# Weight preparations in units 2 to 108 of an attention and MLP kernel, each placed by an offset of its own

## The chip, the cores and the metric

The kernel runs on one core of one Trainium2 chip. The metric is the device time of one execution in microseconds (us). Five engines work side by side, each through its own instructions in order: TensorE (PE in the profile, its weight loads PEld), VectorE (DVE), ScalarE (ACT), GpSimd (POOL) and SyncE (SP), which here only issues DMAs. ACT issues some DMAs too.

## What is computed

An adaLN-conditioned block: attention over the last 512 keys of a cache (32 query heads, 16 key/value heads, head size 128), then a gated MLP. S = 2048 rows, D = 576, F = 4608, all in float32.

```python
x = A_x
mod = (_silu(c) @ w_mod).reshape(c.shape[0], 6, 1, -1)
sa, ca, ga, sb, cb, gb = (mod[:, 0], mod[:, 1], mod[:, 2], mod[:, 3], mod[:, 4], mod[:, 5])
h = _layernorm(x, axis=-1) * (1 + ca) + sa
x = x + ga * _A_ref(h, A_k_cache, A_v_cache, A_wq, A_wo)
h = _layernorm(x, axis=-1) * (1 + cb) + sb
x = x + gb * _B_ref(h, B_W_gate, B_W_up, B_W_down)
...
q = (lambda x, *d: x.transpose(*d))((x @ wq).reshape(B, Sq, Hq, Dh), 0, 2, 1, 3)
scores = jnp.einsum("bhqd,bhkd->bhqk", q, k) * (Dh ** -0.5)
p = _softmax(scores, axis=-1)
o = jnp.einsum("bhqk,bhkd->bhqd", p, v)
...
gate = gate * (lambda x, dt: x.astype(dt))(gate > 0, gate.dtype)
h = gate * up
```

## The kernel before

**Numbers.** Every product is made with operands split in two: a high part (a cast to fp32r, on ACT) and a low part (the difference, on POOL). A product is then three matmuls: high by high, low by high, high by low. So each weight matrix must be *prepared* before it is used.

**Units.** Attention runs as 128 units (UNITS), one for each head and block of 512 query rows; the eight units of a group g share keys and values g and use heads 2g and 2g + 1. In the last five groups each group comes twice, with two blocks each time (VIS). In unit u TensorE does, in this order: 12 score matmuls (s, L496 to L498), 14 matmuls for the query projection of unit u + 1 (qps, L424), a piece of the output projection (wo, L660, 12 matmuls of 288 columns), 12 matmuls of probabilities by values for unit u - 1 (pv, L633 to L635), another piece. The MLP follows.

**The other engines in a unit.** DVE takes maxima of the scores (L501), spreads them (L571), subtracts (L591), makes the low part of the next query (qlo, L480), a partial row sum (ks, L606) and the head's output (L641). ACT makes the next query's high part (qhi, L476), copies a finished piece out of PSUM (acc, L669) and seeds the next one (L693; there is one such PSUM buffer), takes the exponential (L593) and makes the high part of p (hi, L577). POOL finishes the row sum (ks, L609) and makes the low part of p (lo, L600). The output of unit u - 2 is split in high (ohi, ACT L645) and low (olo, POOL L649): at place 0 of an even unit, after place 3 of an odd one. A piece that needs a pair of heads starts at place 6 of the odd unit, behind olo.

**Places.** Everything that isn't part of a unit's fixed order is a step with a time t = 10 u + k: unit u, place k (0 to 9). `run(u, k)` emits all steps up to that time. The program order of each engine's instructions follows from it. Places 0 to 4 come before the first half of the exponential, 5 between the halves, then come ks on DVE and POOL, then 6 and 7, the head's output on DVE, 8, lo on POOL, and 9. A step's time is where it stands in the order, not a clock: an engine reaches it when it is through with what is ahead.

**Preparations.** `prep` makes two or three steps of one: `.l` issues the load on SP into one of two raw buffers, `.g` (output weights only) multiplies by the gate row on DVE (L223), `.c` cuts (ACT L182, POOL L183) into one of three buffers of its kind: wA for q, wB for k and v, wC for o. HOOK allows places 0, 4, 6 and 9, and the load stands a fixed number of hooks ahead of the cut. Group g has q(2g), k(g), q(2g+1), v(g), o(2g), o(2g+1). `park...` are those of the late groups, prepared early and stored to DRAM by `keep` (a DMA from ACT); `again` loads a stored one back on SP. Steps m3 to m5 load and add rows of the modulation (DVE L130), with their own buffers (xm). `w_later` builds sums of the MLP's weights from a layout in DRAM: a load of two tiles, one or more combinations on POOL (L943), between them a reload of the second tile on SP (L933), then a cut (ACT L950, POOL L951 and L953), then a store from ACT (L752). The names are wP60 for P6, first half, and so on; P6 has two combinations. SP also issues many copies that make that layout (wlay, L1459).

Of the kernel before, what the change touches and what calls it, by code (L numbers as in the profile page):

```python
# [23 lines left out]
EPS = 1e-5  # L24
SCALE = float(P) ** -0.5
H2 = D // 2
PLAN = {'a1.st0': -14, 'a1.nm0': -15, 'a1.st1': -14, 'a1.nm1': -15, 'a1.st2': -14, 'a1.nm2': -15, 'a1.st3': -14, 'a1.nm3': -15, 'a1.rs': -15, 'a1.tr0': -15, 'a1.af0': -11, 'a1.tr1': -15, 'a1.af1': -15, 'a1.tr2': -15, 'a1.af2': -15, 'mods': -3}
CFG = {'a0': (('s', 'vvp', 'vvv'), ('m', 'aap', 'avp'), ('w', 'aav')), 'a1': (('w', 'aap', 'vap'), ('m', 'vvp', 'vvv'), ('s', 'avp'))}
PE0, PE1, MLP0 = 4, 1, 8
# [5 lines left out]
def kernel(  # L35
# [106 lines left out]
    def mod_row(j, r, plus):  # L142
# [70 lines left out]
    def prep_out(d, k, src, key, slot=None, at=(None, "wC")):  # L213
# [11 lines left out]
        def cut():  # L225
# [12 lines left out]
    hb = {(qb, d): dr.tile([2, 4, 32, 512] if d == 4 else [P, 512], F32, name=f"hb{qb}_{d}")  # L238
          for qb in range(NQB) for d in range(5)}
# [32 lines left out]
    class LayerNorm:  # L272
# [4 lines left out]
        def stats(self, i):  # L277
# [205 lines left out]
    st_, t5, pt, hi_, lo_, bc, rb, ks_, pvps, done, o, bps = ({} for _ in range(12))  # L483
# [167 lines left out]
    def down_piece(his, los, ws, i, qt, nm, pool=None, seed=None):  # L651
# [3 lines left out]
        for half in range(2):  # L655
            cs = slice(half * H2, (half + 1) * H2)
            n = 0
            for hi, lo, w in zip(his, los, ws):
                for a, b in ((hi, 0), (hi, 1), (lo, 0)):
                    nc.tensor.matmul(ps[:, half, :H2], a[:, sl], w[b][:, cs],  # L660
                                     start=(n == 0 and seed is None), stop=(n == 5),
# [746 lines left out]
    live = {"q": wqs, "k": ks, "v": vs, "o": wos}  # L1408
# [365 lines left out]
```

## Time and profile before

| what | value |
|---|---|
| median of 3 runs | 2860.26 us (2857.57 to 2861.42) |
| the profiled execution | 2857.6 us, span 2855.8 us |
| mean granted TensorE clock | 0.998 |
| instructions | 41174 |
| DMA | 399.57 MB, 140 GB/s on average |

A row of the timeline reads: start in us from the span's start, duration in us, engine, line of the kernel, operation, tile written <- tiles read, shapes, count; in brackets the idle time before it and what ended that. A row of the waits reads: who waited <- for whom, us in total, times, longest. Busy time of TensorE is modelled and matmuls overlap, so rows of 0.39 us start 0.23 us apart.

### The profile page before, as it was taken

Reading aid. Unit: us, or ns where it says so; the run is one execution under the profiler, and the core shown is the slowest. Engines: PE = TensorE matmul, PEld = TensorE weight load, DVE = VectorE, ACT = ScalarE, POOL = GpSimd, SP = SyncE. Lnnn points to the kernel's source line nnn. Section 1 sums busy time; section 2 is a strip of 40 time slices with the busy share of each in tenths; the row PEclk is TensorE's granted clock in tenths of the full one; section 3 lists DMA queues with packets and bytes.
Section 4 is the critical chain, followed back from the end, with each engine's and each line's share of the span. In section 5 each row is a group of like instructions: output and inputs, shape, how many; then the busy total and the mean of one; then the engine's idle time right before and its main releaser. Section 6 shows DMA issues by size and latency. Waiting matters only on the chain.

```text
span 2855.8 us, 41174 instructions
## 1 busy us (share of the span) xinstructions
PE 2815.0 (99%) x15006; PEld 2449.5 (86%) x15006; DVE 2246.8 (79%) x3384; ACT 1476.7 (52%) x2105; POOL 2123.8 (74%) x1564
## 2 busy tenths in 40 slices
PE   6999999999999999999999999999999999999999
PEld 5788888888888888888888888888888888888888
DVE  7899999999889998888889756676677466666666
ACT  5766666666766666666656444444444122222221
POOL 5688888888899989877778766788777356656653
PEclk9999999999999999999999999999999999999999
DMA  4012132222232213312243456666667844444442
GB/s 163 24 45 79 65 106 85 83 82 100 95 104 94 92 62 131 105 70 80 68 155 139 150 213 229 231 240 231 234 234 261 338 165 154 155 155 159 159 154 106
DMA packets 164506, 399.57 MB, mean 140 GB/s; under 512 B 15056, under 2 KB 62160, under 8 KB 164304
## 3 DMA queue, kind: packets, MB, share of 16 engines
q1 hardware_dynamic: 132912, 284.69, 29.9%
q10 hardware_dynamic: 31392, 112.26, 10.0%
q8 instruction: 118, 1.93, 0.3%
q14 instruction: 84, 0.69, 0.1%
HBM read 271.16 MB, written 154.57 MB: 149 GB/s over the span
## 4 chain that ended last, share of the span: by engine, by line
PE 83%; DVE 6%; POOL 5%; issue 2%; ACT 2%; DMA 2%; SPq 0%; ACTq 0%; DVEq 0%; POOLq 0%
PE gu L1016 26%; PE wo L660 12%; PE qps L424 11%; PE md L660 8%; PE st_P L1118 6%; PE s L498 3%; PE s L497 3%; PE s L496 3%; PE pv L635 3%; PE pv L634 3%; PE pv L633 3%; POOL lo L600 2%; DVE t L501 1%; DVE p L591 1%; POOL wop L795 1%
## 5 line engine op out<-in xcount | busy, mean ns | idle before, releaser
L600 POOL TENSOR_TENSOR lo<-p,hi 128x1024 fp32r<-128x1024 f32 x256 | 610.6, 2406 | 1.1 <-ACT hi L577 1.1
L609 POOL TENSOR_TENSOR ks<-ks,p 128x512 f32<-128x512 f32 x256 | 351.7, 1374 | 238.7 <-DVE ks L606 135.5
L501 DVE TRANSPOSE_TENSOR_REDUCE t<-s 128x32 f32<-128x1024 f32 x256 | 313.8, 1239 | 85.9 <-PE s L498 76.6
L1016 PE MATMUL gu<-hop_B,wop 128*128 128x512 f32 x1512 | 375.0, 391 | 0.2 <-POOL wop L795 0.2
L1016 PEld LDWEIGHTS gu<-hop_B,wop 128*128 128x128 f32 x1512 | 274.9, 188 | 51.1 <-POOL wop L795 0.9
L1016 PE MATMUL gu<-hop_T,wop 128*128 128x512 f32 x1260 | 316.1, 391 | 0.0
L424 PE MATMUL qps<-hTa,wA 128*128 128x512 f32 x1288 | 312.9, 394 | 3.1 <-DVE hTa L372 1.6
L660 PE MATMUL wo<-woga,ohi 128*128 128x288 f32 x1472 | 298.8, 295 | 2.0 <-POOL woga L183 1.4
L591 DVE TENSOR_TENSOR p<-s,mb 128x1024 f32<-128x1024 f32 x246 | 290.3, 1219 | 4.2
L424 PEld LDWEIGHTS qps<-hTa,wA 128*128 128x128 f32 x1288 | 244.5, 190 | 56.6 <-DVE hTa L372 3.2
L476 ACT ACTIVATE qhi<-qps 128x512 fp32r<-128x512 f32 x128 | 76.4, 597 | 366.9 <-PE qps L424 358.4
L660 PEld LDWEIGHTS wo<-woga,ohi 128*128 128x128 f32 x1472 | 245.9, 188 | 18.8 <-POOL woga L183 3.4
L1016 PEld LDWEIGHTS gu<-hop_T,wop 128*128 128x128 f32 x1260 | 227.8, 188 | 39.0
L577 ACT CAST hi<-p 128x1024 fp32r<-128x1024 f32 x256 | 259.5, 1042 | 1.5
L660 PE MATMUL md<-wogb,hhi 128*128 128x288 f32 x1272 | 256.9, 295 | 0.4 <-DVE acc L671 0.4
L593 ACT ACTIVATE p<-p 128x1024 f32<-128x1024 f32 x246 | 249.5, 1051 | 13.7 <-DVE p L591 13.4
L671 DVE TENSOR_TENSOR acc<-md,acc 128x576 f32<-128x576 f32 x159 | 119.9, 755 | 160.4 <-PE md L660 159.8
L660 PEld LDWEIGHTS md<-wogb,hhi 128*128 128x128 f32 x1272 | 210.9, 188 | 12.6 <-DVE acc L671 1.4
L1127 DVE TENSOR_TENSOR acc<-st_P,acc 128x576 f32<-128x576 f32 x160 | 121.1, 757 | 127.9 <-PE st_P L1118 127.9
L660 PE MATMUL wo<-woga,olo 128*128 128x288 f32 x736 | 217.8, 296 | 1.3 <-POOL olo L649 1.2
L660 PE MATMUL md<-wogb,hlo 128*128 128x288 f32 x636 | 187.5, 295 | 0.0
L649 POOL TENSOR_TENSOR olo<-rb,ohi 128x512 fp32r<-128x512 f32 x128 | 167.4, 1308 | 15.2 <-ACT ohi L645 15.0
(283 smaller groups left out, 7095.3 us busy)
## 6 DMA issues: line engine op xcount, KB each, us to landing
wop<-wk_P SPq DMA_DIRECT2D x133, 640.0 KB
wk_P<-wop ACTq DMA_DIRECT2D x119, 640.0 KB
wr<-wlay SPq DMA_DIRECT2D x68, 384.0 KB
rogb<-wd SPq DMA_DIRECT2D x68, 288.0 KB
againq<-akq SPq DMA_DIRECT2D x18, 640.0 KB
rwA<-wq SPq DMA_DIRECT2D x32, 320.0 KB
wlay<-wg SPq DMA_DIRECT2D x36, 256.0 KB
roga<-wo SPq DMA_DIRECT2D x32, 288.0 KB
```

What stands on the lines that cost most here:

```text
L424: return [lambda i=i, a=a, b=b: nc.tensor.matmul(ps, a, b, start=(i == 0), stop=(i == n - 1)) for i, (a, b) in enumerate(ops)]
L501: nc.vector.tensor_reduce(t5[u][:, 2 * h:2 * h + 2, :].rearrange("p k b -> p (k b)"), t.rearrange("p k (b j) -> p (k b) j", j=32), axis=AX ...
L577: nc.scalar.copy(hi_[u, h], pt[u, h])
L591: nc.vector.tensor_tensor(p, t, bc[u][:, None, :].to_broadcast([P, 2, 512]), op=ALU.subtract)
L593: nc.scalar.activation(p, p, AF.Exp, bias=0.0, scale=1.0)
L600: nc.gpsimd.tensor_sub(lo_[u, h], pt[u, h], hi_[u, h].bitcast(F32))
L609: nc.gpsimd.tensor_tensor(ks_[u], ks_[u], p[:, j, :], op=ALU.add)
L649: nc.gpsimd.tensor_sub(olo[u], o.pop(u), ohi[u].bitcast(F32))
L660: nc.tensor.matmul(ps[:, half, :H2], a[:, sl], w[b][:, cs], start=(n == 0 and seed is None), stop=(n == 5), skip_group_check=seed is not None)
L1016: nc.tensor.matmul(ps, a, c, start=s not in heir(m) and i == 0 and s not in seeds_of(m), stop=i == len(ops) - 1, skip_group_check=True)
L1118: nc.tensor.matmul(ps[:, j, :H2], x[:, sl], w[:, y, :], start=n == 0 and not second, stop=n == 2, skip_group_check=True)
L1127: nc.vector.tensor_tensor(t, ps[:, :, :H2], t, op=ALU.add)
```

## The change

Each step's time gets an offset of its own from a table OFF of 280 entries, by name; names that aren't in it get 0. So that every step has a name, keep, again, park and the steps of `w_later` are given ones with their weight (and for `w_later` their time). Nothing else changes: the same instructions, buffers and loops. Offsets lie between -24 and +20, that is up to two units and a half; most are between -6 and +6. The last steps moved are at 1060 to 1070.

```diff
+OFF = {'keepo24_0': 10, 'q5.l': 5, 'q5.c': -3, 'parkq25.l': 1, 'q8.c': -9, 'parko25.l': 3, 'parko25.g': -4, 'parko25.c': -3,
...
+ 'o5.g': 2, 'o9.g': -3, 'q11.l': 7, 'q11.c': 12, 'q10.c': 11, 'q12.c': 5, 'o14.l': 7, 'q18.c': -8, 'o17.l': -10, 'o17.g': -10,
...
+ 'wP11.576': -2, 'parkq30.c': -1, 'wP41.656': -1, 'k7.c': -5, 'keepk14_0': 20, 'o16.l': 1, 'o16.g': -6, 'parko28.l': 10,
+ 'parko29.l': 7, 'parko29.c': -4, 'o19.g': -3, 'o20.g': -6, 'o20.c': -9, 'o22.c': 5,
...
+ 'wP60.796': 17, 'wP60.804': 9, 'wP61.824': 14, 'wP61.836': 12, 'wP61.844': 15, 'wP61.856': 3, 'k11.c': -1,
...
+ 'm5.l': -1, 'gb': 1}
...
     def step(name, t, fn, *args):
-        sched.append((t + PLAN.get(name, 0), len(sched), fn, args))
+        sched.append((t + PLAN.get(name, 0) + OFF.get(name, 0), len(sched), fn, args))
...
-        step("keep", t, lambda: keep(key, d[k][2] if key[0] == "o" else
+        step(f"keep{key[0]}{key[1]}_{int(t >= 1000)}", t, lambda: keep(key, d[k][2] if key[0] == "o" else
...
-                step("again", B + t, again, key, live[key[0]], key[1],
+                step(f"again{i}{key[0]}{key[1]}", B + t, again, key, live[key[0]], key[1],
...
-                prep("park", B + t, pr, gap)
+                prep(f"park{key[0]}{key[1]}", B + t, pr, gap)
...
-                step("w.l", t, fn)
+                step(f"w{s}{xx}.{t}", t, fn)
```

The steps that the prediction names, with their times before and after (worked out from the code and the table):

| step | before | after |
|---|---|---|
| parkq30.c, cut of wP11 (name wP11.576) | 576, 576 | 575, 574 |
| parkq31.c, cut of wP41 (wP41.656) | 656, 656 | 656, 655 |
| q10.c, q12.c, q18.c, o22.c | 369, 449, 689, 889 | 380, 454, 681, 894 |
| o9.g, parko25.g, o19.g | 350, 360, 750 | 347, 356, 747 |
| o5.g, o16.g, o20.g | 190, 646, 806 | 192, 640, 800 |
| o20.c | 809 | 800 |
| wP60: two combinations, cut | 796, 804, 816 | 813, 813, 816 |
| wP61: load, two combinations, cut | 824, 836, 844, 856 | 838, 848, 859, 859 |
| k11.c | 860 | 859 |
| q11.c | 386 | 398 |
| keep of k14, k7.c | 513, 540 | 533, 535 |
| o14: load, gate | 559, 566 | 566, 566 |
| o16: load, gate | 639, 646 | 640, 640 |
| parko28: load, gate | 589, 600 | 599, 600 |
| parko29: load, gate | 669, 680 | 676, 680 |

More of the change, by code (lines that the diff above doesn't have):

```diff
@@ L26 @@
 H2 = D // 2
+OFF = {'keepo24_0': 10, 'q5.l': 5, 'q5.c': -3, 'parkq25.l': 1, 'q8.c': -9, 'parko25.l': 3, 'parko25.g': -4, 'parko25.c': -3, 'm4.0.l': -16, 'm4.0.c': -1, 'k3.l': -4, 'parkq26.l': -6, 'o7.l': -1, 'parkq27.l': 12, 'hb.r': -15, 'o5.g': 2, 'keepq27_0': 3, 'v4.c': 2, 'keepk12_0': -6, 'q9.l': -13, 'm4.1.l': -18, 'q10.l': -6, 'parkq26.c': -2, 'q8.l': -14, 'parkv12.l': -3, 'm3.4.l': 1, 'o9.g': -3, 'k3.c': -11, 'm3.3.c': -2, 'o7.g': -3, 'm4.2.l': -5, 'parkk12.l': -18, 'parkk13.l': -6, 'parkk13.c': -10, 'o6.l': 2, 'm3.2.l': 4, 'q6.c': 10, 'm3.1.l': 9, 'o4.c': 4, 'q6.l': 17, 'm3.1.c': -2, 'parko24.g': -1, 'keepk13_0': -12, 'k2.l': 4, 'q11.l': 7, 'k5.c': 12, 'q7.l': 12, 'k4.l': -18, 'v3.l': 5, 'v2.c': -4, 'm4.2.c': -3, 'k4.c': -1, 'keepq25_0': 18, 'keepo25_0': 3, 'm4.4.l': 7, 'keepv12_0': -2, 'v2.l': -4, 'q10.c': 11, 'm3.3.l': 2, 'v4.l': -21, 'keepq26_0': -1, 'o8.l': -1, 'o8.g': 1, 'q9.c': 3, 'o9.l': 3, 'o5.l': -12, 'v5.l': -1, 'o6.c': 14, 'k2.c': 3, 'parkv12.c': -6, 'q4.c': 2, 'm3.2.c': 19, 'q7.c': 8, 'm4.1.c': -2, 'q11.c': 12, 'parkq27.c': 3, 'o7.c': -1, 'parko24.l': -9, 'm4.3.c': 1, 'o6.g': 2, 'm3.pad': 2, 'm4.3.l': -18, 'parko24.c': 13, 'm3.4.c': -1, 'o9.c': -1, 'k6.l': 2, 'k6.c': -3, 'parko28.l': 10, 'parko28.c': -1, 'v7.l': 6, 'wP20.596': -1, 'o13.g': -4, 'wP11.564': 5, 'keepv14_0': 3, 'wP11.576': -2, 'm5.1.l': -13, 'm5.4.c': -2, 'q15.l': -13, 'wP21.604': 10, 'keepk14_0': 20, 'parko26.l': 3, 'parko26.g': -2, 'parko26.c': -5, 'v6.l': -4, 'q14.c': -5, 'parkq29.l': 3, 'o13.l': -18, 'm5.st': -9, 'q16.l': -24, 'm5.4.l': -18, 'keepq29_0': 14, 'o15.l': -12, 'keepo27_0': 11, 'm4.col': -3, 'keepo26_0': 14, 'parkq28.l': -4, 'parkq28.c': 2, 'k7.c': -5, 'parkq29.c': 1, 'q13.l': -6, 'q13.c': -2, 'q16.c': 12, 'm5.2.l': 4, 'v5.c': 1, 'm5.3.l': -7, 'm5.1.c': -3, 'q12.c': 5, 'keepo28_0': 6, 'parkv13.l': -3, 'parkq30.l': -6, 'keepq30_0': -2, 'keepq28_0': 16, 'q12.l': -7, 'm5.0.l': -8, 'q15.c': -4, 'k8.l': -1, 'o12.l': -2, 'o15.g': -4, 'o15.c': -5, 'm5.0.c': -10, 'wP10.546': -19, 'wP10.556': -10, 'o10.c': 4, 'keepv13_0': 8, 'o14.l': 7, 'k7.l': 4, 'parko27.l': 6, 'parkk14.l': -3, 'parkq30.c': -1, 'parkk14.c': -2, 'q14.l': -1, 'parkv13.c': -1, 'o10.l': -9, 'o14.c': -2, 'parkv14.l': 2, 'o11.g': -1, 'o12.c': -2, 'm5.3.c': -1, 'o12.g': 1, 'o11.l': 1, 'parko27.c': -2, 'wP50.744': -7, 'wP60.796': 17, 'wP70.684': 1, 'keepv15_0': 7, 'parkk15.l': 3, 'parkk15.c': -3, 'q17.c': 5, 'wP61.844': 15, 'wP61.824': 14, 'wP61.836': 12, 'o20.l': -14, 'o20.g': -6, 'o20.c': -9, 'parko31.l': -4, 'parko31.g': -3, 'parko31.c': -2, 'parkv15.l': -9, 'wP51.776': -2, 'o21.l': -9, 'o21.g': -1, 'o21.c': -1, 'o19.c': -1, 'parko29.l': 7, 'v10.c': 4, 'wP50.736': -2, 'q22.l': 1, 'q19.l': -12, 'o17.g': -10, 'wP41.644': 2, 'k10.l': -4, 'k10.c': 3, 'wP41.656': -1, 'q19.c': -11, 'q20.c': 6, 'o17.l': -10, 'wP71.704': -3, 'k9.c': -1, 'v9.l': 8, 'v9.c': -1, 'wP71.716': 2, 'k9.l': -8, 'q18.c': -8, 'v10.l': -5, 'wP40.624': 2, 'wP51.756': 2, 'q21.l': 4, 'o19.l': 2, 'v8.l': -5, 'keepk15_0': 5, 'keepo30_0': 7, 'parko30.c': 6, 'o16.c': 1, 'q20.l': -5, 'keepo29_0': 5, 'wP70.676': -2, 'o18.g': 1, 'o16.g': -6, 'parko29.c': -4, 'q18.l': -6, 'wP51.764': 1, 'o19.g': -3, 'keepq31_0': -4, 'q21.c': 6, 'parko30.l': 1, 'parkq31.l': 5, 'o16.l': 1, 'wP21.616': 2, 'o18.c': 2, 'q17.l': 8, 'again15k15': 7, 'v11.l': -6, 'v11.c': -1, 'again13v13': -10, 'again14v14': -3, 'wP31.924': 7, 'again15q31': 5, 'again14o29': 3, 'q23.l': 10, 'q23.c': 4, 'again14o28': 6, 'again13q26': 1, 'again13o26': 1, 'again13o27': 3, 'again15o30': -13, 'again15q30': 12, 'keepo31_0': -5, 'o23.l': -3, 'again13q27': -10, 'again14q28': 12, 'keepo23_0': 1, 'again12q25': -4, 'keepq23_0': 7, 'again14k14': 6, 'again15o31': 1, 'keepo22_0': 16, 'wP31.944': 3, 'q22.c': 3, 'wP31.916': 3, 'wP30.896': -1, 'keepq22_0': 4, 'again16k11': -5, 'o22.l': 7, 'again14q29': -6, 'again12k12': -3, 'keepv11_0': -3, 'again12q24': -11, 'k11.l': -7, 'again16q22': -8, 'o22.c': 5, 'm5.l': -1, 'again13k13': -1, 'again12o25': -11, 'again16q23': 4, 'wP61.856': 3, 'wP31.956': -6, 'k11.c': -1, 'gb': 1, 'wP30.884': 6, 'wP60.804': 9}
```

## The prediction

> **What bounds the kernel now.** I read the page first, for which engine is full, then the waits of TensorE, for what still interrupts it.
>
> ```profile
> PE 2815.0 (99%) x15006; PEld 2449.5 (86%) x15006; DVE 2246.8 (79%) x3384; ACT 1476.7 (52%) x2105; POOL 2123.8 (74%) x1564
> ```
>
> ```profile
> PE wo L660 <- POOL woga L183: 1.4, 3, 0.7
> PE wo L660 <- POOL olo L649: 1.2, 5, 0.5
> PE pv L635 <- POOL lo L600: 1.1, 2, 0.6
> PE s L498 <- DVE qlo L480: 0.9, 2, 0.7
> ```
>
> TensorE is busy 99% of the span, so the change cannot shorten its work; it can only remove interruptions or add some. The few there are come late from POOL or DVE: low parts of weights (L183), of heads' outputs (L649), of probabilities (L600) and of queries (L480). To see how much there is to win, I take from the timeline of TensorE the first score matmul of a unit.
>
> ```profile
> 134.73 0.39 PE L496 MATMUL s<-qhi,kv 128*128 128x512 f32 x1
> 146.56 0.39 PE L496 MATMUL s<-qhi,kv 128*128 128x512 f32 x1
> ```
>
> ```profile
> 745.38 0.39 PE L496 MATMUL s<-qhi,kv 128*128 128x512 f32 x1
> ```
>
> ```profile
> 770.81 0.39 PE L496 MATMUL s<-qhi,kv 128*128 128x512 f32 x1
> ```
>
> ```profile
> 841.87 0.39 PE L496 MATMUL s<-qhi,kv 128*128 128x512 f32 x1
> ```
>
> ```profile
> 866.73 0.39 PE L496 MATMUL s<-qhi,kv 128*128 128x512 f32 x1
> ```
>
> ```profile
> 1307.56 0.39 PE L496 MATMUL s<-qhi,againk 128*128 128x512 f32 x1
> ```
>
> These are the starts of units 7, 8, 58, 60, 66, 68 and 105. Unit 7 is undisturbed: 146.56 - 134.73 = 11.83 us. Units 7 to 104 take 1172.83 us, 98 times 11.83 is 1159.3, so **13.5 us (0.5%) is all that can be won here**. Units 58 and 59 take 25.43, 1.77 too long; 66 and 67 take 24.86, 1.20 too long; the other 10.5 us lie scattered, part of them in a few added matmuls.
>
> **What the change takes away.** No instruction is added or removed; each engine gets the same ones in another order. The cause of the longest pair stands in POOL's timeline.
>
> ```profile
> 745.37 2.67 POOL L609 TENSOR_TENSOR ks<-ks,p 128x512 f32<-128x512 f32 x2 [1.39 <-ACT p L593]
> 748.00 1.57 POOL L183 TENSOR_TENSOR wA<-rwA,wA 128x640 fp32r<-128x640 f32 x1
> 749.53 0.45 POOL L951 TENSOR_TENSOR wb_P<-wa_P,wb_P 32x128 fp32r<-32x128 f32 x1
> 749.95 0.73 POOL L953 TENSOR_TENSOR wa_P<-wa_P,wb_P 128x256 fp32r<-128x256 f32 x1
> 750.64 4.74 POOL L600 TENSOR_TENSOR lo<-p,hi 128x1024 fp32r<-128x1024 f32 x2
> ```
>
> Work at place 6 of a unit (parkq30.c and a cut of w_later, both at 576) comes after ks, which waited 1.39, and ahead of lo: 1.57 + 0.45 + 0.73 = 2.7 us that delay lo. At 575 and 574 it stands ahead of ks and uses that idle time. So units 58 and 59 lose their 1.77. In 66 and 67 only the cut moves ahead (656 to 655), the other stays: I count 1.0. In units 37, 45, 69 and 89 a cut (1.57 for a query's) stands just ahead of olo of an odd unit, which a piece needs at once; 369 goes to 380, 449 to 454, 689 to 681, 889 to 894, all clear of that spot. Gates move from place 0 to 6 or 7 (350 to 347, 360 to 356, 750 to 747), where this trace shows them cheaper:
>
> ```profile
> 638.17 0.75 DVE L223 TENSOR_TENSOR roga<-roga,mrow 128x576 f32<-128x576 f32 x1
> ```
>
> ```profile
> 663.12 1.52 DVE L223 TENSOR_TENSOR roga<-roga,mrow 128x576 f32<-128x576 f32 x1
> ```
>
> The first ran at place 6, the second at place 0 beside POOL's ks. The waits for olo and qlo (0.5 and 0.7 the longest) are what these moves address: I count 0.6 for each of the four cuts and 0.6 for each of the three gates, 4.2 of the 10.5. **Gain 1.77 + 1.0 + 4.2 = 7.0**, between 0 and the 13.5. The Trainium skill, "SBUF — State Buffer", section "SBUF: two separate sides", has DVE instructions with two SBUF inputs and GpSimd's lock one port pair against each other for a whole instruction; the 0.75 against 1.52 agree. By that rule the moves 646 to 640 and 806 to 800, from place 6 to 0, and 190 to 192 lose again what three others gain.
>
> **What it adds.** Four kinds of new waits, read from the offsets.
>
> First, both combinations of P6's first half land on 813 (796 + 17, 804 + 9). The second reads a tile that is loaded again only after the first. POOL stands still for that load, ahead of olo of unit 79 (place 3 of an odd unit).
>
> ```profile
> DMA  0000000000000038686779887720000000000000
> ```
>
> ```profile
> 1109.17 0.32 SPq L933 DMA_DIRECT2D wb_P<-wlay  x1
> ```
>
> ```profile
> 1012.68 1.02 POOL L943 TENSOR_TENSOR wa_P<-wa_P,wb_P 128x384 f32<-128x384 f32 x1
> ```
>
> ```profile
> 1030.33 1.44 POOL L183 TENSOR_TENSOR woga<-roga,woga 128x576 fp32r<-128x576 f32 x1
> 1031.72 1.31 POOL L649 TENSOR_TENSOR olo<-rb,ohi 128x512 fp32r<-128x512 f32 x1
> ```
>
> The first line is the DMA view from 1109.10 to 1112.00 us, 40 slices of 0.0725 us, with one such load issued at 1109.17: the last busy slice ends at 1111.1, so 2.0 us. In unit 81 POOL was free of lo at 1030.33, and olo ended at 1033.03, already a little late for its piece. Now: 1030.33 + 1.02 + 2.1 + 1.02 + 1.31 = 1035.8, 2.7 later (o20's cut is gone from there, 809 to 800). The earlier gate lets lo end up to 0.4 sooner: **2.3**, between 0 and 2.7.
>
> Second, P6's second half has its last combination and its cut both on 859. ACT's cast waits for POOL, and qhi and both copies that free TensorE's only wo buffer queue behind it on ACT.
>
> ```profile
> 1081.46 0.51 ACT L950 CAST wb_P<-wa_P 128x384 fp32r<-128x384 f32 x1
> ```
>
> ```profile
> 1090.28 0.64 ACT L693 COPY wo<-acc 128x576 f32<-128x576 f32 x1
> ```
>
> ```profile
> 1089.93 1.28 POOL L183 TENSOR_TENSOR kv<-rkv,kv 128x512 fp32r<-128x512 f32 x1
> ```
>
> ```profile
> 1092.10 0.42 PE L660 MATMUL wo<-woga,ohi 128*128 128x288 f32 x2
> ```
>
> POOL reaches k11's cut 1.18 sooner than 1089.93 (the 0.45 and 0.73 are no longer ahead), then 1.28 and 1.02: 1091.05. ACT's five (0.51 for the cast, some 0.62 for each of ohi, qhi and the two copies) then take 3.0: 1094.05. The piece wanted its buffer at 1092.10: **1.9**, between 0 and 3.0.
>
> Third, three single cuts come late. q11's (386 to 398) follows ks of unit 39, while TensorE needs it in the second qps matmul of unit 40:
>
> ```profile
> 529.06 2.65 POOL L609 TENSOR_TENSOR ks<-ks,p 128x512 f32<-128x512 f32 x2 [1.68 <-DVE ks L606]
> ```
>
> ```profile
> 532.90 0.84 PE L424 MATMUL qps<-hTa,wA 128*128 128x512 f32 x3
> ```
>
> ```profile
> 751.56 6.70 DMA wk_P<-wb_P
> ```
>
> 529.06 + 2.65 + 1.57 = 533.28 against some 533.1, and ks itself may be 0.4 slower. k7's cut (535) needs a buffer whose store is issued only at 533 (513 before), and the last row, of the chain of waits, shows a store taking 6.70. o5's gate (192) now stands between DVE's maximum and the subtraction. I take 0.4 + 0.5 + 0.5 = **1.4**, between 0 and 5.
>
> Fourth, **late loads**. From load to gate there are 7 or 11 places before; now 0 for o16 (640, 640) and o14 (566, 566), 1 for parko28 (599, 600), 4 for parko29 (676, 680). SP issues a load when one of two raw buffers is free, so what matters is the time from that release to the use.
>
> ```profile
> 864.08 1.44 POOL L183 TENSOR_TENSOR woga<-roga,woga 128x576 fp32r<-128x576 f32 x1
> ```
>
> ```profile
> 865.54 0.35 SPq L190 DMA_DIRECT2D rwA<-wq  x1
> ```
>
> ```profile
> 867.29 1.54 DVE L223 TENSOR_TENSOR roga<-roga,mrow 128x576 f32<-128x576 f32 x1
> ```
>
> ```profile
> DMA  1111111111311111189962111139999811111111
> ```
>
> o17's cut ends at 865.52 and the next load goes out at 865.54; in the changed kernel that load is parko29's, and its gate's turn is at 867.29, 1.75 later. A quiet load takes at least the 2.0 above. The last line is the DMA view of 758.3 to 768.3 with a load of that kind beside a layout copy: busy until 8.0. DVE waits for the gate's load with the row maxima queued behind it, then ACT and TensorE. Each of the four costs between 0 and 6; with about 1 us of slack on DVE and mostly quiet queues I take **3.0** for all, between 0 and 15.
>
> **Sum.** -7.0 + 2.3 + 1.9 + 1.4 + 3.0 = +1.6 on the profiled execution's 2857.6, 2859.2; that execution lies 2.7 under the median of the three runs, 2860.26, so **2862** as a median. What can be told from no change is 0.2%, 5.7 us.
>
> **Rivals.** *The new waits stay hidden* (faster): POOL waited 1.39 before ks, so a queue that runs ahead of its place could absorb the reload and the cast at 859. Only the gain and a little of the rest stay: -7.0 + 1.0, 2854. For it: the offsets at 574, 575 and 655 hit just the places that the trace shows full. Against it: 2.1 us of standing still is more than the 1.39.
>
> *Loads land behind layout copies* (slower): one mechanism, the four short loads above. It decides as soon as the DMA queue is as full as at 758 us, 8.0 instead of 2.0: then each gate is some 4 us late, 3 past the slack, 12 instead of 3.0 in all: 2871. For it: two of the four fall between 730 and 770 us, where that load was seen. Against it: the load at 865.54 had little beside it.
>
> *The moves do nothing* (same): SP's loads go out when a buffer is released, wherever they are written, so many offsets change nothing; then 2860. Against it: cuts and gates do move on their engines.
>
> A gap of TensorE can also cost clock: the Trainium skill, "TensorE: Matmul & The Clock Gate", section "What's actually happening", halves the clock after an idle window of about 3.4 us. By that rule unit 81, if its wait grew past 3.4, would lose up to another 1.7 us by my estimate; the trace shows a granted clock of 0.83 only early:
>
> ```profile
> 40.00:60.00 20.00, 15.49 (x55) 11.59 (x54) 16.15 (x36) 7.82 (x11) 11.45 (x9) 0.83 0.13 42
> ```
>
> **How the numbers follow.** The forecast has 0.45 (its own range 2855 to 2869: faster 0.08, same 0.24, slower 0.13), hidden waits 0.24 (faster 0.19, same 0.05), late loads 0.27 (slower), no effect 0.04 (same). So faster 0.27, same 0.33, slower 0.40. The range takes in most of both outer rivals: 2850 (gain 10) to 2876 (late loads at 12, 81 and 86 at their upper ends).
>
> **What would show it.** Right: units 58, 59, 37, 45 and 69 at about 11.83; unit 81 long with POOL waiting for a load of wb_P between two L943; unit 86 long with ACT's L950 waiting for POOL. Late loads show as DVE's L223 waiting for a DMA of roga. Wrong: POOL idle nowhere at 81, no wait of ACT at 859, or loss in units where I name none; and a time outside 2850 to 2876.

## The result and the profile after

| | before | after |
|---|---|---|
| median of 4 runs on one chip | 2860.84 us (2857.57 to 2862.18) | 2885.37 us (2883.13 to 2886.36) |
| profiled execution, its span | 2855.8 | 2883.7 |
| units 7 to 104 in the profile | 1172.8 | 1193.2 |
| units 0 to 6 | 99.3 | 100.5 |

The change makes the kernel slower: ratio 1.0093, 95% interval 1.0081 to 1.0106, some 25 us. The forecast was 2862, with a range from 2850 to 2876. One of the four executions of a later experiment, e13, ran at a granted clock of 0.751 and took 3498.43 us; e13's time below is the median of the other three, and nothing is said of its units, as that one was the profiled one.

The page of the changed kernel, its totals (all lines of the source stand one lower than before, L660 is now L661):

```profile
span 2883.7 us, 41156 instructions
PE 2824.0 (98%) x15006; PEld 2455.3 (85%) x15006; DVE 2240.8 (78%) x3384; ACT 1476.4 (51%) x2105; POOL 2123.7 (74%) x1564
```

The span grew by 27.9 us but PE's busy time by only 9: PE idles more, and part of its work runs longer. Units 7 to 104 account for 20.4 of the 27.9, units 0 to 6 for 1.2, and the part from unit 127 on for 6.1 (1282.0 against 1275.9). That last part takes 1279.1 to 1280.3 in profiles of three kernels with none of the offsets, or k7's two alone (e7, e8 and e10 below), so most of the 6.1 isn't the change; the section on e6 says where it comes from. The waits of PE, us in all, how many, and the longest:

```profile
PE wo L661 <- ACT wo L694: 6.9, 6, 2.3
PE s L499 <- DVE qlo L481: 5.0, 5, 1.9
PE wo L661 <- POOL olo L650: 4.0, 3, 3.1
```

Before, the wait for qlo was 0.9 in all, that for olo 1.2, and that on ACT:

```profile
PE wo L660 <- ACT wo L693: 0.3, 1, 0.3
```

To place them, the distance from one unit's first score matmul to the next one's (L496, now L497) was taken for every unit of every profile; 11.83 is undisturbed. Only groups that differ are shown; the right column is units 7 to 104 together, in the profile after from

```profile
136.12 0.39 PE L497 MATMUL s<-qhi,kv 128*128 128x512 f32 x1
```

to

```profile
1329.36 0.39 PE L497 MATMUL s<-qhi,againk 128*128 128x512 f32 x1
```

```
                     19-20  31    32-34  45-46  54     57     58-59  60-61  63     66-67  81-82  86-87  7-104
before               24.01  11.83  35.48  25.07  11.83  11.83  25.43  23.75  11.83  24.87  24.07  23.64  1172.83
after                24.26  11.83  43.04  23.65  15.86  11.83  24.51  28.23  12.66  25.82  28.60  26.27  1193.24
```

Six places carry the loss: 32 to 34 (7.56), 54 (4.03), 60 and 61 (4.48), 66 and 67 (0.95), 81 and 82 (4.53), 86 (2.63). The waits of DVE, ACT and POOL in stretches around the first three and the last two, one row from each, in this order:

```profile
DVE roga L224 <- DMA roga<-wo: 3.8, 1, 3.8
...
ACT kv L183 <- DMA rkv<-kv: 5.3, 1, 5.3
...
DVE roga L224 <- DMA roga<-wo: 4.8, 1, 4.8
...
POOL wa_P L944 <- DMA wb_P<-wlay: 3.0, 1, 3.0
...
ACT wb_P L951 <- POOL wa_P L944: 6.8, 1, 6.8
```

Each time an engine stands in front of a transfer or of POOL, with TensorE's inputs queued behind it. In the first stretch DVE's L131 had already waited 2.9 for a row of the modulation (wm). Why the first of them is late shows in SP's timeline (start, duration, instruction):

```profile
425.08 5.50 SPq L139 DMA_DIRECT2D wm<-wmod  x1
430.62 0.58 SPq L1460 DMA_DIRECT2D wlay<-wu  x1
431.25 11.14 SPq L1460 DMA_DIRECT2D wlay<-wg  x2
442.49 5.25 SPq L220 DMA_DIRECT2D roga<-wo  x1
```

An issue on SP takes 0.3 to 0.6 us when nothing is in its way; here two copies of the layout took 11.14 to issue and o8's load, behind them, another 5.25. The DMA view of 425 to 465 us (40 slices of 1 us) says what the transfers did meanwhile:

```profile
DMA  7111116511111111111111169411116311116511
GB/s 251 48 48 49 50 47 144 212 48 48 50 48 48 49 48 48 48 48 49 48 48 48 48 120 388 154 48 67 51 47 203 124 48 48 50 48 171 212 49 48
```

Long stretches at 48 GB/s with the DMA engines little more than a tenth busy: a copy of 256 KB needs 5.3 us, though one slice of this view reaches 388. DVE shows the price:

```profile
449.26 0.67 DVE L607 TENSOR_TENSOR ks<-p 128x512 f32<-128x512 f32 x1
453.72 1.94 DVE L224 TENSOR_TENSOR roga<-roga,mrow 128x576 f32<-128x576 f32 x1 [3.79 <-DMA roga<-wo]
455.59 0.68 DVE L642 TENSOR_TENSOR rb<-pv,rb 128x512 f32<-128x512 f32 x1
```

The load was issued from 442.49 on and could be used at 453.7, 11 us later. DVE's L642, needed for the next head's output, came behind it. At unit 54 the same with a cut on ACT:

```profile
701.80 1.05 ACT L594 ACTIVATE p<-p 128x1024 f32<-128x1024 f32 x1
708.15 0.62 ACT L183 CAST kv<-rkv 128x512 fp32r<-128x512 f32 x1 [5.30 <-DMA rkv<-kv]
708.68 1.05 ACT L594 ACTIVATE p<-p 128x1024 f32<-128x1024 f32 x1
```

The single DMA packets of this load (k7, issued from 694.97), counted from the trace:

```
what                 packets x bytes    first start - last end (us)
layout copy          256 x 1024         692.96 - 699.99
k7's load            112 x 2048         702.20 - 703.43
layout copy          256 x 1024         700.49 - 707.16
k7's load, the rest   16 x 2048         707.17 - 707.81
```

Seven eighths of the load are there at 703.4; the last 16 packets start only when the copy has ended. So the copy seems to run on a few DMA engines that this load, of 128 rows, needs for its last eighth. The outermost dimension of a copy is its two tiles. That fits the Trainium skill, "DMA: Bandwidth & Descriptors", section "Why a DMA increments its semaphore by 16 and not by 1": a DMA is cut over as many engines, up to 16, as divide the slowest dimension of both its sides, the lowest-numbered ones; two here. The trace names no engine, but 112 packets and 16 agree with fourteen and two. A store on ACT's queue, of k14 (`akk<-kv`, issued at 698.92), is split in the same way: 112 packets by 701.17, the last 16 from 702.61 to 704.15.

The last term is TensorE's clock. Four stretches of the profile after; the last three numbers of a row are the granted clock, the DMA share and GB/s:

```profile
448.00:472.00 24.00, 20.51 (x94) 16.86 (x95) 19.41 (x35) 14.66 (x20) 17.42 (x11) 0.93 0.36 122
708.00:732.00 24.00, 21.82 (x108) 18.81 (x108) 18.91 (x34) 18.03 (x25) 20.91 (x14) 0.93 0.26 93
790.00:812.00 22.00, 19.41 (x93) 16.18 (x93) 18.59 (x33) 13.67 (x19) 13.26 (x11) 0.92 0.18 61
1048.00:1070.00 22.00, 18.89 (x90) 16.30 (x90) 15.46 (x26) 11.10 (x15) 16.13 (x12) 0.92 0.24 73
```

A granted 0.93 over 24 us is 1.7 us of work lost. The trace's clock records show in each of the four one piece of 3.41 us at half clock; before, units 7 to 104 have none. So of the 20.4 us lost there, an estimated 6.8 (four times 1.7) are clock and not the gap itself. Two experiments told of below, e4 and e18, bear this out at unit 81: PE waits 2.8 for olo in both, and the stretch from 1030 to 1058 us is, in e4 and then in e18,

```profile
1030.00:1058.00 28.00, 25.24 (x131) 21.72 (x130) 22.42 (x38) 16.79 (x24) 22.21 (x16) 1.00 0.21 65
```

```profile
1030.00:1058.00 28.00, 25.25 (x125) 21.81 (x124) 21.69 (x38) 15.52 (x21) 20.55 (x15) 0.94 0.22 65
```

The same 25.2 us of busy PE hold 131 matmul records at full clock and 125 at 0.94, and units 81 and 82 together take 26.69 in e4 and 28.09 in e18, 1.40 more.

Why one gap brings such a piece and another doesn't can be read from the same records. Within a profile the half-clock pieces start whole multiples of 3.41 us apart, so the span can be cut into windows of 3.41 us that don't move with the work. Four of them, with the busy time of PE after the length: at unit 54 and at unit 86 in the profile after, then at unit 81 in e4 and in e18:

```profile
710.11:713.52 3.41, 1.23 (x8) 0.81 (x7) 0.73 (x2) 3.38 (x6) 3.33 (x4) 1.00 0.27 103
1112.88:1116.29 3.41, 2.07 (x14) 2.03 (x15) 1.15 (x3) 3.38 (x5) 0.90 (x2) 1.00 0.82 237
1038.97:1042.38 3.41, 1.60 (x10) 1.22 (x8) 2.79 (x6) 2.78 (x4) 1.72 (x2) 1.00 0.52 152
1036.81:1040.22 3.41, 0.96 (x7) 0.69 (x5) 2.18 (x4) 2.79 (x4) 1.97 (x2) 1.00 0.59 171
```

The first and the last are followed by half clock, the other two aren't. In units 7 to 104 of the 18 profiles other than e13's, each of the 19 windows at full clock in which PE was busy for 1.54 us (45%) or less is followed by half clock, and none with 1.60 (47%) or more is. The same wait can fall into one window or be shared by two.

### The profile page after: what moved, and what is told of

Its sections match the earlier page's. It is cut to its first block, busy times and chain, and to the rows that moved or that the text cites. A ratio compares the mean times of both kernels' runs of the same rounds, so it can differ in the third digit from the quotient of the medians.

```text
span 2883.7 us, 41156 instructions
## 1 busy us (share of the span) xinstructions
PE 2824.0 (98%) x15006; PEld 2455.3 (85%) x15006; DVE 2240.8 (78%) x3384; ACT 1476.4 (51%) x2105; POOL 2123.7 (74%) x1564
## 4 chain that ended last, share of the span: by engine, by line
PE 63%; POOL 2%; DVE 2%; DMA 1%; ACT 1%; issue 1%; ACTq 0%; DVEq 0%; POOLq 0%
PE gu L1017 26%; PE md L661 8%; PE wo L661 6%; PE st_P L1119 6%; PE qps L425 6%; PE s L499 2%; PE s L498 2%; PE s L497 2%; PE pv L636 2%; PE pv L635 2%; PE pv L634 2%; POOL lo L601 1%; DVE ws L824 1%; POOL wop L796 0%; POOL ks L610 0%
## 5 line engine op out<-in xcount | busy, mean ns | idle before, releaser
L661 PE MATMUL wo<-woga,ohi 128*128 128x288 f32 x1472 | 299.2, 296 | 7.3 <-ACT wo L694 6.9
L661 PEld LDWEIGHTS wo<-woga,ohi 128*128 128x128 f32 x1472 | 246.1, 188 | 24.9 <-ACT wo L694 9.7
L661 PE MATMUL md<-wogb,hhi 128*128 128x288 f32 x1272 | 257.5, 295 | 2.4 <-DVE acc L672 2.4
L661 PEld LDWEIGHTS md<-wogb,hhi 128*128 128x128 f32 x1272 | 211.3, 188 | 15.1 <-DVE acc L672 4.0
L661 PE MATMUL wo<-woga,olo 128*128 128x288 f32 x736 | 218.2, 297 | 4.1 <-POOL olo L650 4.0
L661 PE MATMUL md<-wogb,hlo 128*128 128x288 f32 x636 | 187.9, 295 | 0.0
```

The costliest lines, as they stand in the source:

```text
L661: nc.tensor.matmul(ps[:, half, :H2], a[:, sl], w[b][:, cs], start=(n == 0 and seed is None), stop=(n == 5), skip_group_check=seed is not None)
```

## The experiments

Each edit is a difference to the changed kernel, or, where said, to the one before. The theories: **A**, loads land late because moved loads hold SP, and copies and later loads pile up; **B**, each stall comes from the step's own load, issued too late; **C**, places of gates and cuts on the engines. A2 and D2, further down, are about the copies themselves.

**e1_P6.** The entries `wP60.*` and `wP61.*` taken out of OFF.

> The changed kernel with the six offsets of P6's second and third pieces undone (796, 804, 824, 836, 844, 856 back at their regular places). If the reload of P6's buffer at 813 and the two steps at 859 alone make units 81, 82 and 86 long: unit 81 falls from 15.78 to about 12.0 us, 82 from 12.82 to 11.83, 86 from 14.44 to 11.83, and the time from 2885.4 to 2878 (-7.2). If the neighbours moved beside them (o20, v10, q22, k11) share the blame, those units stay over 12.5 and the time stays above 2881.

Measured 2874.95, ratio 1.0056 (1.0041 to 1.0071): units 81 and 82 24.16, 86 11.83, no other unit by more than 0.5. That is 7.1 us in the units, 10.4 between the medians. The rows for the two places in the profile after show the mechanism that the prediction described:

```profile
1044.85 1.02 POOL L944 TENSOR_TENSOR wa_P<-wa_P,wb_P 128x384 f32<-128x384 f32 x1
1048.87 0.99 POOL L944 TENSOR_TENSOR wa_P<-wa_P,wb_P 128x384 f32<-128x384 f32 x1 [2.99 <-DMA wb_P<-wlay]
1049.82 1.27 POOL L650 TENSOR_TENSOR olo<-rb,ohi 128x512 fp32r<-128x512 f32 x1
```

```profile
1110.73 0.51 ACT L951 CAST wb_P<-wa_P 128x384 fp32r<-128x384 f32 x1 [6.83 <-POOL wa_P L944]
1111.15 0.62 ACT L646 CAST ohi<-rb 128x512 fp32r<-128x512 f32 x1
1111.67 0.59 ACT L477 ACTIVATE qhi<-qps 128x512 fp32r<-128x512 f32 x1
```

POOL stands 2.99 between the two combinations, olo follows; ACT stands 6.83, and ohi, qhi and the copies follow.

**e2_early, e3_late, e4_q9v4.** Loads back at their regular places: 34 that the change issues earlier, 39 that it issues later, and two of the early ones alone.

```
-'q9.l': -13, 'v4.l': -21,        (e4; e2 and e3 the same for their lists)
```

> The changed kernel with 34 of the loads that it issues earlier back at their regular places (those whose buffer's next reader stays at least 9 places behind); gates, cuts, combs and keeps stay as changed. Theory A (a load that stands in SP's stream before its raw buffer is free holds SP, so layout copies and later loads pile up behind it and land late): the stalls of units 32 to 34 (7.5 us), 54 (4.0) and 60 to 63 (5.0) go, the time falls by 12 to 16 us to about 2871. Theory B (loads issued too late in their own step): these stalls stay, 2883 to 2887. Theory C (places of gates and cuts on the engines): the stalls stay too.

> The changed kernel with all 39 loads that it issues later back at their regular places. Theory B: the stalls at units 54 (k7) and 60 (parko28) go, 9 us, to about 2877; unit 32 stays. Theory A: little changes at unit 32 and 54; within 4 us of 2885. Theory C: nothing changes.

> The changed kernel with two loads alone back at their regular places: q9 (283 to 296) and v4 (289 to 310). In the profile after, q9's load held SP from unit 28.9 to 30.3 (399 to 414 us). Theory A: with them back the copies behind are spread again, the stalls of units 32 to 34 (7.5 us) go, everything else stays: 2878. Theory C or B: 2885, stalls of units 32 to 34 unchanged.

```
                     31     32-34  54     57     58-59  60-61  66-67  81-82  7-104    time, ratio
after                11.83  43.04  15.86  11.83  24.51  28.23  25.82  28.60  1193.24
e2_early             11.83  35.48  15.41  11.86  26.82  24.46  27.28  26.75  1183.22  2872.62  1.0049 (1.0033-1.0066)
e3_late              11.83  44.96  12.07  18.29  24.34  23.66  25.61  26.67  1190.31  2882.35  1.0088 (1.0072-1.0105)
e4_q9v4              18.35  35.48  15.65  11.85  24.47  24.44  25.75  26.69  1186.08  2879.76  1.0078 (1.0061-1.0095)
```

No theory holds in its plain form. Early loads put back cure 32 to 34 (A) but not 54; late loads put back cure 54 and 61 (B) but open unit 57 with 6.5; two loads cure 32 to 34 and open unit 31 with 6.5. Units 60 and 61 shrink to 24.4 in e2 and e4 too, where the load they wait for (parko28's) stays where the change put it. C falls for these stalls: no gate or cut was put back. The new stalls are late transfers again, in e3 and in e4:

```profile
ACT wb_P L951 <- DMA wa_P<-wlay: 5.7, 1, 5.7
```

```profile
ACT wA L183 <- DMA rwA<-wq: 10.1, 1, 10.1
```

Moving loads moves the stall to whichever load meets the copies.

**e8_k7.** The kernel before with k7's load at 534 and its cut at 535, no other offset.

> The kernel before with the two offsets of k7 alone: load 530 to 534, cut 540 to 535. If the short distance of one place between them makes unit 54 long by itself: unit 54 goes from 11.83 to about 15.5 us, the rest stays, +4 us. If only the queue of copies that other moved loads have built up makes it late (theory A in its strict form): unit 54 stays under 12.5.

One run: 2861.03; unit 54 took 11.83. A distance of one place is harmless by itself: SP issues a load when a buffer is free. Here k7's load went out at 685.46, behind two copies that made its issue 4.00 long, and its cut came only at 696.65, without a wait. The store of k14 stood at its old place in this run, so it says nothing of that.

**e5_layact, e7_before_layact.** The layout copies issued by ACT in place of SP, in the changed kernel and in the one before.

```
-             lambda ab=ab: nc.sync.dma_start(*ab))
+             lambda ab=ab: nc.scalar.dma_start(*ab))
```

> The changed kernel with all offsets kept; only the 152 layout copies of gate and up weights (256 KB each, up to 5.3 us of issue on SP) go out through ACT's queue. Theory A (loads land late because they stand behind copies in SP's queue): units 32 to 34, 54, 60, 61 return to 11.8 to 12.3 us, 81, 82 and 86 stay long; about 2869 (-16). Theory D (the 16 DMA engines or the memory behind them are what is late, whatever the queue): those units stay long, 2883 to 2888, or longer by what ACT now loses in issuing.

> The kernel before with the layout copies on ACT's queue and no offset. It has only one wait of PE for a late load to lose, and 0.5 us per unit at a few others: within 3 us of 2859 if the copies cost ACT nothing; slower by some 0.6 us for each copy issued in the attention if ACT's queue is held as SP's was (up to +20 us).

e5: 2882.13, ratio 1.0085 (1.0072 to 1.0099). Units 32 to 34 are 35.48 again, but 54 stays at 14.93 and 60 and 61 at 26.80, and 45 and 46 are new with 29.82. So SP's queue was the limit at 32 to 34. At 60 the load stays late although no copy is issued on SP; at 54 another transfer has taken its place. The wait of DVE from 778 to 798 us in e5, and k7's cut on ACT there:

```profile
DVE roga L224 <- DMA roga<-wo: 3.5, 1, 3.5
```

```profile
706.24 0.62 ACT L183 CAST kv<-rkv 128x512 fp32r<-128x512 f32 x1 [4.27 <-DMA akk<-kv]
```

k7's load had landed by 695.3; the cut waited for the store of k14 out of its buffer, issued at 697.57, whose last 16 packets ran from 703.97 to 705.76, right behind a copy (698.54 to 704.01) on the same queue.

Units 86 and 87 took 29.38 in e5. e7: 2864.16, ratio 1.0020 (1.0011 to 1.0029), 5 over the expected 2859; no unit of 7 to 104 changed by more than 0.5, and together they take 1173.16.

**e9_spread, e10_before_spread.** The copies with their 128 rows outermost, in both kernels.

```
-[(wlay[f:f + 2, j, :, xx, 0:256], src[f:f + 2, :, 256 * j:256 * j + 256])
+[(wlay[f:f + 2, j, :, xx, 0:256].rearrange("f p n -> p f n"),
+  src[f:f + 2, :, 256 * j:256 * j + 256].rearrange("f p n -> p f n"))
```

> The changed kernel with all offsets kept; the layout copies of 256 KB are written with their 128 rows ahead of their two tiles, so that one copy should be cut over more DMA engines (in the profile after, a copy's 256 packets of 1 KB took 5.3 to 7 us, and the last 16 packets of the load of k7 waited for them: 112 packets by 703.4, 16 from 707.2 to 707.8 us). Theory A2 (the copies fill the DMA engines that every load needs for its last eighth): a copy lands in about 1 us, units 32 to 34, 54, 60 and 61 go back to 11.8 to 12.5 us, 81, 82, 86 stay; 2868 (-17). Theory D2 (memory bandwidth, or the order in SP's queue): those units stay, 2883 to 2888.

> The kernel before with the same form of the copies and no offset. Its units lose 0.4 to 1.4 us at 35 to 37, 45, 58, 59, 66, 67, 69, 75, 81, 89; by theory A2 only what is left of late loads goes, at most 3 us: 2856 to 2859. By D2 2859.

```
                     19-20  32-34  54     58-59  60-61  66-67  81-82  86-87  7-104
e9_spread            24.51  35.48  11.83  24.02  23.65  24.78  28.72  26.26  1176.22
e10_before_spread    28.92  35.48  11.83  24.86  23.69  24.86  24.07  23.64  1176.94
```

e9: 2865.22, ratio 1.0021 (1.0011 to 1.0030). With all offsets kept, the stalls at 32 to 34, 54, 60 and 61 are gone and 66 and 67 are as before, 20 us between the medians; what P6 costs stays. But e10 was slower than before, 2866.43, 1.0022 (1.0012 to 1.0032), where it should have gained: units 19 and 20 lost 4.9. The issues of copies between 130 and 300 us, in the kernel before and then in e10, say why:

```profile
wlay<-wu SPq DMA_DIRECT2D x7, 256.0 KB
wlay<-wg SPq DMA_DIRECT2D x6, 256.0 KB
```

```profile
wlay<-wu SPq DMA_DIRECT2D x30, 256.0 KB
wlay<-wg SPq DMA_DIRECT2D x29, 256.0 KB
```

The source orders PE, DVE, ACT and POOL by hand (L52) and leaves SP's order to the build; with the other form of the copies the build put 59 of them there instead of 13. From 271.6 to 294.0 us 5,422 packets of 1 KB ran, 248 GB/s, 1.06 us a copy in place of 5.3; now too many at once, and ACT waits:

```profile
ACT p L594 <- DMA wlay<-wu: 3.4, 1, 3.4
```

In e9 the build did the same (70 such copies between 130 and 300 us), so it removes them from units 32 to 61 as well as spreading them: 44 copies of 256 KB are issued there in the changed kernel and none in e9, where 44 smaller ones (128 and 144 KB) stand in their place. What it shows is that the offsets of loads are harmless there without the copies of 256 KB in their old form; which of the two is enough it can't say. e16 below says more.

**e11_spread_P6, e12_wins_spread, e6_wins.** e11: copies as in e9, and P6's offsets undone. e6: the kernel before with only 15 offsets: the ten that the prediction counted as gains, the load of q18, and four more gates moved the same way. e12: e6 with the copies as in e9.

```
+OFF = {'parkq30.c': -1, 'wP11.576': -2, 'wP41.656': -1, 'q10.c': 11, 'q12.c': 5, 'q18.c': -8, 'q18.l': -6,
+       'o22.c': 5, 'o7.g': -3, 'o9.g': -3, 'parko25.g': -4, 'o13.g': -4, 'o15.g': -4, 'o19.g': -3, 'parko31.g': -3}
```

> The changed kernel with the copies' form changed and the six offsets of P6 undone. If losses by late loads (17 us) and by P6 (7 us) are all there is, and the gains at units 35 to 37, 45, 58, 75, 89 (4 us) stay: 2859 to 2861, or 2856 if the two other stalls by loads (unit 63, 66) go too. If the offsets cost something else: over 2865.

> The kernel before with 15 of the offsets alone, those behind the gains that the prediction counted: cuts parkq30 575, P1 574, P4 655, q10 380, q12 454, q18 681 (its load 673), o22 894, and seven gates 3 or 4 places earlier. In the profile after, units 35, 36, 37, 45, 58, 59, 75 and 89 were shorter by 4.7 us together. If these gains don't hang on the other moves: those units alone shorten and the time falls by 4 to 5 us, ratio 0.998. If they are only had together with the shifted loads: ratio 1.000.

> The kernel before with the 15 offsets of e6_wins and the copies' form changed. Attention in the profile of e6_wins was 3.3 us shorter than before while the time was the same to 2.5 us; the copies take up to 3 us more off: 2853 to 2856, ratio 0.998, if the rest of the program takes the gain over; 2858 if it gives it back.

e11: 2861.81, ratio 1.0008 (0.9999 to 1.0017); units 7 to 104 in 1169.74, 3.1 shorter than before. e6: 2858.53, ratio 1.0002 (0.9993 to 1.0010) over 12 runs; units 7 to 104 in 1169.69. e12: 2864.07, 1.0016 (1.0007 to 1.0025), with e10's stall at 19 and 20. So the gains are real in the units, some 3 us, and no median of the whole kernel shows them. In e6's profile the part behind the attention was 4 us longer than in the profile before (1279.9 against 1275.9 from the start of unit 127). One addition there explains most of it:

```profile
1974.36 6.07 DVE L824 TENSOR_TENSOR wr<-wr,wr 128x768 f32<-128x768 f32 x1
1980.36 0.74 DVE L672 TENSOR_TENSOR acc<-md,acc 128x576 f32<-128x576 f32 x1
1981.62 0.94 DVE L824 TENSOR_TENSOR ws<-wr,wr 128x768 f32<-128x768 f32 x1
```

One operation of the same shape takes 0.94 in one place and 6.07 in another, and PE waits 2.4 for the accumulation behind it. POOL's timeline shows why: five of its instructions follow each other without a gap from the first of these two to the second, whose end is at 1979.61.

```profile
1974.29 0.75 POOL L795 TENSOR_TENSOR wop<-wr,wop 32x256 fp32r<-32x256 f32 x1 [1.84 <-ACT wop L794]
1978.90 0.71 POOL L795 TENSOR_TENSOR wop<-wr,wop 32x256 fp32r<-32x256 f32 x1
```

The addition starts 0.07 after the first of them and ends at 1980.43, 0.82 after the fifth. In the 18 profiles other than e13's, all 611 additions of this shape that take over 1.3 us end 0.81 to 0.83 after the end of a POOL instruction; each profile has several of 4.0 to 4.8. So DVE stands still while POOL works on, and the time depends on which of the two comes first. The 6.07 is no effect of the change: the profiles of e7, e8 and e10, kernels with none of the offsets but k7's two in e8, have it too, and those of before and e9 don't. Against e8 (span 2859.2), e6's profile (2856.5) is 2.7 shorter. Whether the other executions of the kernel before have it is not known, so where the gain goes in the medians stays open.

**e13_man, e15_before_man_spread, e16_man_spread_P6, e17_wins_man_spread.** SP's stream in the order of the steps.

```
-engines={ET.PE, ET.DVE, ET.Activation, ET.Pool}
+engines={ET.PE, ET.DVE, ET.Activation, ET.Pool, ET.SP}
```

> The changed kernel with all offsets and the slow form of the copies; SP's stream is put in the order of the steps (the source orders PE, DVE, ACT and POOL by hand, and leaves SP's order to the build, which put three copies right ahead of the load of o8 in the changed kernel, one in the one before). If that order makes the pile: units 32 to 34 go back to 11.83, 54 and 61 get shorter, 2870 to 2878. If copies on few DMA engines are enough at any order: units 32 to 34, 54, 61 stay long in sum (over 12 us), 2880 to 2890.

> The kernel before with the copies' form of e9 and e10 and SP in the order of the steps, no offset. In e10 the build had moved 60 of 72 copies ahead of 300 us (13 before), and units 19 and 20 lost 4.9 us behind them. If that pile was the cause, units 19 and 20 are 12.2 and 11.83 again and the time is 2858 to 2861; if the copies' form itself slows something there, it stays at 2866.

> The changed kernel with the six offsets of P6 undone, the copies' form changed and SP in the order of the steps. If the shifted loads cost only by the copies that they meet: no stall over 0.9 us in units 7 to 104 beside that of unit 39, 2856 to 2859, ratio 0.999. If early loads hold SP whatever the copies: new stalls, over 2862.

> The kernel before with the 15 offsets of e6_wins, the copies' form changed and SP in the order of the steps. e6_wins had 3.3 us less attention than before; with e12's stall at units 19 and 20 (4.9 us) gone: 2855 to 2858, ratio 0.999. If SP's order by the steps makes loads late: over 2861.

All missed in time: 2917.03 (ratio 1.0207, 1.0191 to 1.0223), 2882.84 (1.0083, 1.0067 to 1.0099), 2877.63 (1.0065, 1.0053 to 1.0078) and 2877.48 (1.0065, 1.0052 to 1.0078). Where e13 loses its time stays open. In e15 and e17 the attention up to unit 118 did what was expected: units 19 and 20 are 24.0 in e15 against e10's 28.9, and units 7 to 104 take 1171.9 and 1169.6. In e16 they take 1170.4; units 66 and 67 are 26.25 there, so stalls over the 0.9 expected stay. But e16 answers what e9 left open. In units 32 to 61 it issues 42 copies of 256 KB (44 in the changed kernel), ten of them in units 30 to 34 as there, all in the spread form and with every offset kept but P6's; units 32 to 34 take 35.48, 54 takes 11.83, 60 and 61 take 23.68. So the stalls go without taking the copies away. SP's order changed with it, and e13, which has that order with the old form, has no profile at full clock; its time, 39 us over e16's with the form and P6's offsets (10 us in e1) as the only differences, speaks against the order as the cure. e15, e16 and e17 lose 19 to 20 us in units 119 to 123 (79.5 to 81.0, before 60.7), nearly all of it in 119 and 123, where the order of the steps puts stores that wait ahead of loads on SP. In e17, the waits of ACT from 1455 to 1505 us and of SP from 1430 to 1505:

```profile
ACT hy_B L894 <- DMA hk_B<-hz_B: 10.6, 1, 10.6
```

```profile
SPq L249 <- ACT lfb L344: 40.9, 2, 22.8
```

There the order that the build gives SP is 19 us better than that of the steps.

**e18_two.** The changed kernel with two of its 280 offsets undone.

```
-'k7.c': -5, 'parko28.l': 10,
```

> The changed kernel with two offsets undone: the cut of k7 at 540 again in place of 535, and the load of parko28 at 589 again in place of 599 (with it the build puts one layout copy fewer ahead of that load). Theory A2: k7's last packets came 12.8 us after SP began to issue the load and 5.3 us after ACT asked for them; with the cut 5 places (5.9 us) later unit 54 goes from 15.86 to about 11.9 us; unit 61 goes from 15.54 (and 60 from 12.69) to under 12.5; units 32 to 34, 81, 82, 86 stay; 2877 (-8). If the waits hang on other moved steps as well, 54 or 61 stay over 13.

2874.96, ratio 1.0062 (1.0045 to 1.0079); unit 54 11.83, units 60 and 61 23.65, and 32 to 34 43.05 as in the changed kernel. SP's stream, as built, around parko28's load differs from the changed kernel's in one place:

```
 L934  wa_P<-wlay
-L1460 wlay<-wg x2
-L220  roga<-wo
+L1460 wlay<-wg
+L220  roga<-wo
+L1460 wlay<-wg
```

One copy fewer ahead of the load: the stall is gone. The 10 places in the source don't make the load itself earlier: it goes out 2.3 us ahead of unit 60's first matmul in both (778.17 and 780.47 in the profile after, 772.61 and 774.94 in e18). Behind two copies its first 112 packets ended at 780.55 and its last 16 at 784.93; behind one, all 128 were there at 774.99. k7's cut, 5 places (5.9 us) later, covers the 5.3 that ACT had waited but for 1.50, which unit 54 hides. For k7, e8 shows that its two offsets cost nothing without the other moves; for parko28 no such run was made.

## Why the prediction was wrong

**What could be won** (13.5 at most) was not contradicted: no run brought units 7 to 104 under 1169.6, 3.2 less than before.

**Gains, 7.0 predicted.** The seven units with a moved cut or gate that it priced and that shortened (35, 36, 37, 45, 69, 75, 89) gave 4.06 together against 4.2. Units 58 and 59 gave 0.92 of 1.77 (1.27 in e6). Units 66 and 67 grew by 0.95 in place of 1.0 less, with loads late there (0.53 less in e6). Not every cause was right: in e6 unit 75 stays at 12.49, 69 grows, 35 gains only 0.12 of its 0.48 and 45 only 0.49 of its 1.40, so those gains come mostly from other moves than the ones named, and that the sum fits the 4.2 is in part luck. The gates' 0.75 and 1.52, quoted for places 6 and 0, differ by who came first: at 638.17 DVE started 0.23 ahead of POOL's ks, at 663.12 it started 0.39 behind it. The three gates moved the other way (646 to 640, 806 to 800, 190 to 192) cost nothing in units 64 and 80 and 0.24 in unit 19. And the rule used for the four cuts, no cut just ahead of olo in an odd unit, was not turned on the change: q17's goes from 626 to 631 and stands right ahead of olo in unit 63 in POOL's timeline, and that unit is 0.83 longer; no run took it back alone.

**P6, 2.3 and 1.9 predicted.** The mechanisms were right at both places, and e1, with P6's six offsets undone, leaves none of the loss there. The sizes: POOL's wait for the reload 2.99 (2.1 assumed), so 2.6 to 2.7 for units 81 and 82 where the clock held, the top of the range given, and 4.53 in the profile after with the clock. Unit 86: 2.63, inside the range of 0 to 3.0.

**Single cuts, 1.4 predicted.** q11 0.48 (0.4), o5 0.24 (0.5). k7 cost 4.03, with the load last to land in the profile after (707.81). The store of k14 that the prediction named was real but hidden: it landed at 704.2, 1.35 after ACT was ready for the cut (702.85), and in e5 it alone held the cut, for 4.27.

**Late loads, 3.0 predicted: the step that failed.** They cost 17, outside even the 0 to 15 given for them: 7.56 at 32 to 34, 4.03 at 54, 4.48 at 60 and 61, and 0.95 at 66 and 67, where ACT waited for a load of keys with its copies for TensorE behind it:

```profile
866.07 0.62 ACT L183 CAST kv<-rkv 128x512 fp32r<-128x512 f32 x1 [5.37 <-DMA rkv<-kv]
```

Two things were wrong in it. The steps were picked by their distance in the source, so o14 and o16 were named, which cost nothing, and o8 (load 318, gate 327) and the row of the modulation ahead of it were not. And the queues were called mostly quiet, though the DMA view quoted there has a load beside a copy. That view was also misread: the burst that ends at 8.0 is mostly a store (112 packets of 4 KB from 765.01 to 766.42), and the load's own packets are 112 from 762.54 to 763.87 and the last 16 from 766.44 to 767.54, 9.2 us after its issue. So the pattern that made the stalls was in the trace before. The rival that took this price came nearer: DVE's waits of 3.79 and 4.78 for gates agree with its "some 4 us late". That its 12 for four gates comes near the 17 is in part luck: of its four, o14 and o16 cost nothing, parko29's gate waited 2.00 without making its unit longer, and o8's gate, k7 and the keys at 66 were not among them. What decided here is how many copies are under way ahead of a load or beside it (e18, e5) and their form (e16), which no distance in the source shows.

**The range** was narrower than its terms. The terms named for its upper end give 2871 + 0.4 + 1.1 = 2872.5, not 2876, and the single bounds under "What it adds" sum to 2.7 + 3.0 + 5 + 15 = 25.7, which with no gain makes 2886, where the measured median lies.

**The clock** was left out of the sum, as no wait of 3.4 us was forecast. Shorter ones were enough: a wait of 2.2 at unit 54 brought a half-clock piece, and so did 0.9 and 1.9 within 3.5 us at unit 33; 2.3 at unit 86 brought none, and 2.8 at unit 81 brought one in e18 and none in e4. The Trainium skill, "TensorE: Matmul & The Clock Gate", section "What's actually happening", has the clock fall after an idle window of about 3.4 us. The length agrees: the half-clock pieces are 3.41 us. The condition, read as a window that is idle throughout, does not: here 45% busy or less was enough.

The sum for units 7 to 104, predicted +1.6, measured +20.4: late loads 17.0 (3.0), P6 7.2 (4.2), the single cuts other than k7 0.7 (0.9), not foreseen 1.4 (units 52 and 63), gains 5.5 (7.0), which makes 20.8; the remaining units took 0.4 off. The clock's 6.8 are inside these terms.

## What to carry to other kernels

A load that the program issues early lands when the queue and the DMA engines let it: before moving loads or their readers, list what stands ahead of each load in the queue as built, and price it by what one such transfer takes in the trace (here 5.3 us a copy). A copy that takes far longer than other transfers of its size in the same trace is worth a look at its outermost dimension, since here it delayed the last part of loads and stores beside it as well. A stall of TensorE should be priced with the half-clock piece that may follow it.

## What was not expected of the hardware

- A copy of 256 KB with two outermost rows ran at 48 GB/s, 5.3 us; with 128 outermost rows at 248 GB/s, 1.06 us a copy, and then a burst of them kept the DMA engines over 90% busy and made units 19 and 20 4.9 us longer.
- Seven eighths of a 256 KB load were there at 703.4 us, the last 16 packets at 707.8.
- A gap of TensorE of 2.2 to 2.8 us costs up to another 1.7 us at half clock in some profiles and nothing in others; it comes where a window of 3.41 us has PE busy for 45% or less.
- An addition of 128x768 on DVE takes 0.94 us, or up to 6.08 when POOL's instructions follow each other without a gap: it then ends some 0.82 after one of them.

No version measured here is faster than the one before by more than its interval: e6 is the nearest, 1.0002 (0.9993 to 1.0010).
